# Attention's masked scores times v: two 64-column products side by side become one 128-column product

## The chip, the cores and the metric

The kernel runs on one core of one Trainium2 chip. The metric is the device time of one execution in microseconds (us). The kernel before took 642.28, 639.79 and 642.13 us in three runs, median 642.13; one more execution, taken by the hardware profiler, took 640.24 us and is the one the rows below come from. Engines are named as the profile names them: PE is TensorE's matmuls, PEld its weight loads, DVE VectorE, ACT ScalarE, POOL GpSimd, SP the engine that issues most DMAs.

## What is computed

Batch 4, 8 heads, 768 positions, head dimension 64. Attention goes in blocks with a decay of its own per head, and its output feeds a low-rank mixer with a two-layer perceptron:

```python
for b in range(nb):
    qb, kb, vb = (q[:, :, sl], k[:, :, sl], v[:, :, sl])
    intra = np.einsum('bhic,bhjc->bhij', qb, kb) * Dmask[None]
    intra = np.einsum('bhij,bhjd->bhid', intra, vb)
    inter = np.einsum('bhid,bhde->bhie', qb * lam_pow[None], kv_state)
    out[:, :, sl] = intra + inter
    kv_state = lam_block * kv_state + np.einsum('bhsd,bhse->bhde', kb_dec, vb)
...
h = xt @ U @ V
u = x + h.transpose(0, 2, 1)
ch = np.maximum(u @ w_ch1, 0.0) @ w_ch2
return (u + ch).astype(np.float32)
```

All of it is float32. The line that matters here is the second one of the loop: the masked scores times v.

## The kernel before

**Stages.** Attention takes blocks of 128 positions instead of the reference's 64 (same result, other grouping): 4 batches x 6 blocks = 24 steps, numbered s, with c = s % 6 the place in the batch. It lasts for about the first 118 us of the span. Then come the first layer of the perceptron and its second layer, long rows of matmuls with 128 columns of weights and 512 moving columns. Some of the mixer's work (mix, turn) and the preparation of the first weights are woven into the steps of attention.

**Order.** The order of the work in attention is written out by hand: a list of pieces for each step, run one after the other under a manual schedule. TensorE does its instructions in that order. A step, as TensorE sees it from step 7 on: the second half of earlier mixer work, the transposes of the next block's q and k (L416), intra (L514), state (L486), inter (L525), some mixer work (L618), the next step's scores (L463). Up to step 6 state comes ahead of intra. The last block of a batch (c = 5) has no state, the first (c = 0) no inter.

**The pieces around the change.**
- scores, L463: for each of 8 heads a product with 128 columns of weights and 128 moving columns over 64 rows; the two heads of a pair (x) lie in the two row halves of the array. The result goes to two banks of the matmul memory.
- masked, L472: VectorE multiplies the scores by the decay mask, one instruction for each x, into the tile sm: partitions are the positions j that are summed over, columns the 128 positions i of the block.
- intra, L514: masked scores times v, into the tile px. The weights are columns of sm, the moving operand is v of the head, 64 columns wide. The sum goes over 128 rows. The 128 positions i are taken in two halves, t = 0 and 1, each its own product with 64 columns of weights and its own 64 partitions of px: 2 x 4 x 2 = 16 products in a step.
- state, L486: keys times v for the running state, 8 products with 64 columns of weights over 128 rows.
- inter, L525: scaled queries times the state, added to px: 16 products of 64 rows by 64 columns, in quarters of the array.
- L531: ScalarE copies px out when inter is done.

The profile gives the part of the array that a matmul uses as rows*columns: 128*64 for L514 and L486, 64*64 for L525, 64*128 for L463 and L416, 128*128 for the perceptron.

A float32 product leaves two weight loads and two matmuls in the trace. So L514's 16 products in 24 steps are the 768 loads and 768 matmuls of its rows; transposes and the matmuls of type fp32r leave one of each.

Of the kernel before, what the change touches and what calls it, by code (L numbers as in the profile page):

```python
# [18 lines left out]
def kernel(  # L19
# [28 lines left out]
    nc = tc.nc  # L48

    B, H, S, D = q.shape  # L50
    HP = H // 2
# [258 lines left out]
    def two_banks(name, tag):  # L310
        return psf.tile([P, 2, N], FP32, tag=tag, name=name)
# [83 lines left out]
    half = [slice(0, D), slice(D, P)]  # L395
# [110 lines left out]
    def intra(s):  # L506

        st[s]["px"] = both = two_banks("px", "px")
        px = both[:, :, 0 : HP * D].rearrange("p x (a e) -> p x a e", a=HP)
        sm, vr, alone = st[s]["sm"], raw[s, "v"], s % NT == 0  # L510
        for x in range(2):
            for a in range(HP):
                for t in range(2):
                    nc.tensor.matmul(  # L514
                        out=px[half[t], x, a, :], lhsT=sm[:, x, a, half[t]],
                        rhs=vr[:, 2 * a + x, :], start=(a == 0), stop=(alone and a == HP - 1),
                    )

    def inter(s):

# [214 lines left out]
    def load_next(name, engine=nc.sync):  # L735
# [4 lines left out]
    run = {  # L740
        "prep": prep, "fade": fade, "scores": scores, "masked": masked, "inter": inter,
        "intra": intra, "state": state,
        "low": low, "low_rows": low_rows, "next_of_low": next_of_low, "mix": mix, "turn": turn,
        "mixed": mixed, "store": store, "next_v": next_v, "split": lambda s: splits.pop(s)(),
# [727 lines left out]
```

## Time and profile before

| what | value |
|---|---|
| median of three runs | 642.13 us |
| the profiled execution | 640.24 us |
| its span, first to last instruction | 638.5 us |
| TensorE matmuls busy, whole span | 628.4 us, 5197 records |
| weight loads busy, whole span | 529.0 us, 5197 records |
| VectorE, ScalarE, GpSimd busy | 463.0, 334.3, 147.0 us |
| granted TensorE clock | 1.0 |
| L514: matmul record, median | 222 ns |
| L514: idle time of PE just before it | 1.8 us in all |

The span is what the records cover; the execution's own time is 1.74 us longer. Busy time of matmuls is the union of their records, which overlap: a record of 222 ns does not mean that the next one starts 222 ns later. The start of one record to the start of the next of its kind says how fast they go.

### The profile page before, as it was taken

How to read it: one execution, taken by the hardware profiler on the slowest of the kernel's cores; microseconds unless marked ns; L12 is line 12 of the kernel's file. 1: busy time of each engine (PE TensorE's matmuls, PEld its weight loads, DVE VectorE, ACT ScalarE, POOL GpSimd, SP SyncE). 2: the span in 40 equal slices, each digit the busy share in tenths (PEclk: the TensorE clock that was granted, in tenths of full speed). 3: DMA queues.
4: the chain of work that ended last, by engine and by line, in shares of the span. 5: the costliest groups of instructions: out<-in, count | busy, mean ns of one | idle time of the engine just before them, and what ended most of it. 6: DMA issues, size and time to landing. Idle time of an engine off the chain costs nothing.

```text
span 638.5 us, 13622 instructions
## 1 busy us (share of the span) xinstructions
PE 628.4 (98%) x5197; PEld 529.0 (83%) x5197; DVE 463.0 (73%) x740; ACT 334.3 (52%) x615; POOL 147.0 (23%) x125
## 2 busy tenths in 40 slices
PE   8899999999999999999999999999999999999997
PEld 7888989888888888888888878888888888888886
DVE  6756778757888788797888799685674755855844
ACT  4675767445777777778777654232322322323220
POOL 4475959100000000000566500030110300300300
PEclk9999999999999999999999999999999999999999
DMA  9979996347798888855776696362363363532521
GB/s 230 244 186 269 233 248 163 135 175 268 260 354 281 280 306 290 292 195 190 250 232 229 227 332 216 112 225 95 113 216 99 127 203 93 190 131 99 182 83 66
DMA packets 141955, 129.61 MB, mean 203 GB/s; under 512 B 82562, under 2 KB 99970, under 8 KB 141890
## 3 DMA queue, kind: packets, MB, share of 16 engines
q1 hardware_dynamic: 116768, 122.32, 59.4%
q10 hardware_dynamic: 25122, 6.42, 4.5%
q8 instruction: 41, 0.67, 0.4%
q14 instruction: 24, 0.20, 0.1%
HBM read 79.04 MB, written 49.28 MB: 201 GB/s over the span
## 4 chain that ended last, share of the span: by engine, by line
PE 95%; ACT 2%; issue 1%; DMA 1%; DVE 1%; DVEq 0%; ACTq 0%
PE pz L958 24%; PE pz L1314 14%; PE pz L1312 14%; PE pd L1316 13%; PE z L958 4%; PE px L514 4%; PE pss L463 4%; PE p L958 3%; PE pz L889 2%; PE d L958 2%; PE px L525 2%; PE pqk L416 2%; PE c L958 2%; PE pkv L486 1%; PE pd L900 1%
## 5 line engine op out<-in xcount | busy, mean ns | idle before, releaser
L1296 ACT ACTIVATE m<-rm 128x512 fp32r<-128x512 f32 x96 | 60.6, 631 | 174.6 <-PE pd L1316 136.6
L1297 DVE SCALAR_TENSOR_TENSOR m<-rm,m 128x512 fp32r<-128x512 f32 x96 | 71.6, 747 | 82.1 <-ACT m L1296 82.1
L958 PE MATMUL pz<-u_hl,w 128*128 128x512 f32 x448 | 110.3, 389 | 0.0
L1312 PE MATMUL pz<-w_hl,m 128*128 128x512 f32 x264 | 102.7, 389 | 0.0
L1314 PE MATMUL pz<-w_hl,m 128*128 128x512 f32 x264 | 102.7, 389 | 0.0
L1316 PE MATMUL pd<-w_d,m 128*128 128x512 f32 (+1 forms) x267 | 101.4, 387 | 0.0
L958 PEld LDWEIGHTS pz<-u_hl,w 128*128 128x128 f32 x448 | 84.1, 188 | 17.4
L285 POOL TENSOR_TENSOR w<-w 128x512 fp32r<-128x512 f32 x29 | 40.5, 1415 | 211.4 <-DVE w L279 197.1
L1298 DVE SCALAR_TENSOR_TENSOR m<-m 128x512 fp32r<-128x512 f32 x96 | 74.9, 780 | 3.1
L1344 POOL TENSOR_TENSOR o<-o,u 128x512 f32<-128x512 f32 x20 | 29.8, 1519 | 199.1 <-DVE o L1340 199.1
L958 PE MATMUL pz<-u_d,w 128*128 128x512 f32 x224 | 59.9, 389 | 0.0
L1316 PEld LDWEIGHTS pd<-w_d,m 128*128 128x128 f32 x267 | 49.9, 188 | 10.3
L1312 PEld LDWEIGHTS pz<-w_hl,m 128*128 128x128 f32 x264 | 49.6, 188 | 10.3
L1314 PEld LDWEIGHTS pz<-w_hl,m 128*128 128x128 f32 x264 | 49.6, 188 | 10.2
L958 PEld LDWEIGHTS pz<-u_d,w 128*128 128x128 f32 x224 | 42.0, 188 | 8.8
L1312 PE MATMUL pz<-w,m 128*128 128x512 f32 x120 | 46.7, 389 | 0.0
L1316 PE MATMUL pd<-w,m 128*128 128x512 f32 x120 | 46.7, 389 | 0.0
L1314 PE MATMUL pz<-w,m 128*128 128x512 f32 x120 | 46.7, 389 | 0.0
L965 ACT ACTIVATE pz<-pz 128x512 f32<-128x512 f32 x56 | 32.5, 581 | 26.4 <-PE pz L958 26.4
L472 DVE TENSOR_TENSOR sm<-pss,mask 128x512 f32<-128x512 f32 x48 | 30.9, 686 | 19.8 <-PE pss L463 19.8
L969 ACT ACTIVATE r<-pz 128x512 f32<-128x512 f32 x56 | 33.2, 595 | 12.0 <-PE pz L958 11.4
L196 DVE SCALAR_TENSOR_TENSOR sc<-words,sc 128x512 uint32<-128x512 uint32 (+2 forms) x34 | 23.8, 700 | 17.6 <-ACT sc L178 17.6
(140 smaller groups left out, 1119.5 us busy)
## 6 DMA issues: line engine op xcount, KB each, us to landing
r_d<-r SPq DMA_DIRECT2D x96, 256.0 KB, 2.9
rm<-r_d SPq DMA_DIRECT2D x96, 256.0 KB, 2.6
words<-in_moe_w_ch_dram SPq DMA_DIRECT2D x30, 512.0 KB, 5.1
wf<-forms_d SPq DMA_DIRECT2D x56, 128.0 KB, 2.9
u_d<-x_nat SPq DMA_DIRECT2D x24, 256.0 KB, 4.2
u<-u_d SPq DMA_DIRECT2D x24, 256.0 KB, 4.5
qraw<-in_q_dram SPq DMA_DIRECT2D x23, 256.0 KB, 4.6
out_dram<-o SPq DMA_DIRECT2D x23, 256.0 KB, 2.0
```

The costliest lines, as they stand in the source:

```text
L285: engine.tensor_tensor(out=st["third"], in0=st["low"].bitcast(FP32), in1=st["hi"].bitcast(FP32), op=ALU.subtract,)
L472: nc.vector.tensor_tensor(out=sm[:, x], in0=pss[:, x], in1=mask[:, x], op=ALU.mult)
L958: nc.tensor.matmul(out=out, lhsT=weights, rhs=moving, start=start and i == 0, stop=i == len(pieces) - 1, skip_group_check=not start,)
L965: nc.scalar.mul(acc, acc, 1.0 + E)
L969: nc.scalar.mul(r, acc, 4096.0)
L1296: nc.scalar.activation(out=m[:, 0], in_=r, func=AF.Relu, scale=NEAR)
L1297: nc.vector.scalar_tensor_tensor(m[:, 1], r, 0.0, hi, ALU.max, ALU.subtract)
L1298: nc.vector.scalar_tensor_tensor(m[:, 2], hi, E, low, ALU.mult, ALU.subtract)
L1312: nc.tensor.matmul(out=pz, lhsT=m[:, 0, cols], rhs=hi, start=first, stop=False)
L1314: nc.tensor.matmul(out=pz, lhsT=m[:, 1, cols], rhs=low, start=False, stop=end)
L1316: nc.tensor.matmul(out=pd[:, part], lhsT=m[:, 2, cols], rhs=third[:, part], start=first, stop=end, skip_group_check=part.stop != C,)
L1344: nc.gpsimd.tensor_tensor(out=o, in0=o, in1=u, op=ALU.add)
```

## The change

The loop over the two halves t goes. Each product takes all 128 columns of sm for its head as weights and writes all 128 partitions of px. The moving operand, the order over x and a and the start and stop marks stay. A step has 8 products where it had 16; each uses the whole array (128*128) where each used one column half (128*64).

```diff
         for x in range(2):
             for a in range(HP):
-                for t in range(2):
-                    nc.tensor.matmul(
-                        out=px[half[t], x, a, :], lhsT=sm[:, x, a, half[t]],
-                        rhs=vr[:, 2 * a + x, :], start=(a == 0), stop=(alone and a == HP - 1),
-                    )
+                nc.tensor.matmul(
+                    out=px[:, x, a, :], lhsT=sm[:, x, a, :],
+                    rhs=vr[:, 2 * a + x, :], start=(a == 0), stop=(alone and a == HP - 1),
+                )
```

Nothing else of the kernel is changed; in the changed kernel the line of the product is L513, and later lines count one less.

## The prediction

> **What bounds the kernel now.** I read first how busy TensorE is by stage, then the chain of waits in the stage that holds the change, then that stage's weight loads and matmuls in order of time, and last the loads' durations by line. The first view gives busy time and records of each engine in four stretches (the third lies inside the second):
>
> ```profile
> core 0: us, PE busy (x) PEld busy (x) DVE busy (x) ACT busy (x) POOL busy (x), PEclk, DMA share, GB/s
> 0.00:118.00 118.00, 111.98 (x2873) 102.38 (x2877) 83.19 (x160) 73.17 (x168) 76.72 (x76) 1.00 0.88 215
> 118.00:372.00 254.00, 254.00 (x1174) 209.70 (x1167) 204.30 (x337) 184.70 (x322) 40.53 (x29) 1.00 0.75 256
> 220.00:310.00 90.00, 90.00 (x399) 74.53 (x398) 77.06 (x122) 69.67 (x118) 2.72 (x2) 1.00 0.76 257
> ```
>
> Attention is the first 118 us. TensorE is idle there for 118.00 - 111.98 = 6.0 us, and for nothing in the 254 us behind it. So whatever attention ends later moves the end of the kernel by as much; only those 6.0 us can swallow a delay. The chain of waits of this stretch, by line, says whose work it is:
>
> ```profile
> by line: PE px L514 19.7%; PE pss L463 19.5%; PE px L525 10.9%; PE pqk L416 9.3%; PE pkv L486 7.1%; PE pm L618 5.2%; DMA qraw<-in_q_dram 4.6%; issue 4.1%; PE pm L675 3.1%; PE pp L541 2.6%; PE idle L401 2.4%; PE pz L889 1.9%; ACT vp L772 1.6
> ```
>
> The line that is changed, L514, is on it with 19.7% of 118 us = 23 us, 0.97 us in each of 24 steps. What sets its pace shows in the order of time, weight loads (PEld) first, then matmuls (PE); each row is a run of like records with its start, its length and its count:
>
> ```profile
> 37.33 0.97 PEld L463 LDWEIGHTS pss<-qt,kt 64*128 64x128 f32 x16 [0.28 <-ACT kt L422]
> ...
> 44.07 1.01 PEld L514 LDWEIGHTS px<-vraw,sm 128*64 128x64 f32 x32
> 44.99 0.55 PEld L486 LDWEIGHTS pkv<-vraw,ks 128*64 128x64 f32 x16
> 45.62 0.56 PEld L525 LDWEIGHTS px<-kv,qs 64*64 64x64 f32 x32
> ```
>
> ```profile
> 35.57 0.69 PE L486 MATMUL pkv<-vraw,ks 128*64 128x64 f32 x16
> ...
> 37.33 1.16 PE L463 MATMUL pss<-qt,kt 64*128 64x128 f32 x16
> ...
> 41.93 1.05 PE L463 MATMUL pss<-qt,kt 64*128 64x128 f32 x16
> ...
> 45.05 0.64 PE L486 MATMUL pkv<-vraw,ks 128*64 128x64 f32 x16
> 45.62 0.69 PE L525 MATMUL px<-kv,qs 64*64 64x64 f32 x32
> ```
>
> L514's 16 float32 products of a step leave 32 loads and 32 matmuls, two records for each product. Products t=0 and t=1 use the two column halves of the array, and single records show the two 7 ns apart: they run side by side. 32 loads are 16 pairs; a load lasts 138 ns, so the pairs follow each other every (1010 - 138) / 15 = 58 ns. L525 puts four at once into quarters and keeps the same rhythm: (560 - 135) / 7, less the 20 ns over which four start, is 58 ns. So neither the number of records nor that of loads sets the 58 ns, and halving the number of products alone wins nothing. L463, with 128 weight columns in each of two row halves, goes at (970 - 188) / 7 = 112 ns.
>
> The loads' durations by line (minimum, median, maximum in ns):
>
> ```profile
> L541 PEld LDWEIGHTS pp<-x_nat,u_w x192: 106/110/110, 33.0 to 118.9; 128*32 128x32 f32 x192
> L525 PEld LDWEIGHTS px<-kv,qs x640: 129/135/135, 14.0 to 114.9; 64*64 64x64 f32 x160
> L514 PEld LDWEIGHTS px<-vraw,sm x768: 132/138/138, 9.1 to 114.3; 128*64 128x64 f32 x192
> L463 PEld LDWEIGHTS pss<-qt,kt x384: 182/188/330, 6.0 to 112.1; 64*128 64x128 f32 x192
> ```
>
> 32, 64 and 128 columns take 110, 138 and 188 ns: 0.78 to 0.88 ns for each further column, and the rows hardly count (L525 and L514). Where a group begins afresh, single records show the second load of a half 28, 55 and 109 ns behind the first for 32, 64 and 128 columns. So the weight path is held some 0.85 ns per column, 109 ns for 128; separate halves or quarters load at the same time.
>
> **The change, part by part.** (1) A product now has 128 columns of weights on the whole array, and 8 are left of 16: 16 records of each kind where 32 stood. They no longer pair up, so the row of 16 slots stays 16 slots long. A slot now holds a load of 128 columns against matmul work that took 58 ns. Its cost is not in this trace: no float32 load of 128 columns is followed by a matmul of only 64 moving columns on the full array. The low end is 58 ns (the load wholly hidden, L514's own rhythm), the high end 188 ns (the load's whole record, nothing hidden). I take L463's 112 ns: same type and columns, half the rows, which do not count in the durations; and 109 ns is the hold seen by itself. Of a step's 16 slots 15 are intervals: 15 x (112 - 58) = 0.81 us.
>
> A rule of the Trainium skill would make it worse. TensorE: Matmul & The Clock Gate, Part 3, The mechanism, lists as seen in traces that a weight load overlaps a matmul in flight only when it goes to another row group; on the whole array there is no other. By it a slot would be a load behind a matmul. This trace contradicts it: between 220 and 310 us every load and matmul takes the whole array, and loads are in flight for 74.53 of 90.00 us while matmuls are busy for all 90.00. With the overlap the sum stands as above; without it, it is the third rival's.
>
> (2) Changing the array's division costs time. From L486's first matmul at 45.05 to L525's at 45.62 are 0.57 us, where 8 pairs at 58 ns need 0.47: 0.09 us (0.094 by single records) lost in going over. The first interval of the new group is longer too: L486 lasts 0.69 us entered from another division and 0.64 entered from L514, 0.05 more; L463, with 128 columns, 1.16 against 1.05, 0.11 more. L514 and L486 shared one division (128*64) and now do not. In the 20 steps that have both, whichever comes first, that is one more crossing: 0.09 + 0.05 = 0.14 us, x 20 = 2.8 us. In every step the group of L514 begins with a load of 128 columns: 0.11 for 0.05, 0.06 us.
>
> (3) Nothing else moves: the DMAs, the semaphores waited for, VectorE's L472 and ScalarE's L531 stay in order. Behind L514 on TensorE stand L486 or L525, then the rest of the step, so all of it starts later. The second half of L514 waits for the second half of the masked scores; it comes later now, so that wait can only shrink. These engines have room: 83.19, 73.17 and 76.72 us busy of 118.
>
> Sum: 24 x (0.81 + 0.06) + 2.8 = 23.7 us.
>
> (4) What is given back. Part of the 6.0 us goes: two waits for q's loads early on, whose landing times don't follow TensorE, and the waits that the profile gives to nobody, 3.8 us of "issue" ahead of L514, L416, L525, L463 and L486. These may shrink because a quarter fewer records per microsecond are issued there. The first two are:
>
> ```profile
> 11.82 0.35 PEld L416 LDWEIGHTS pqk<-ident,qraw 64*128 64x128 f32 x8 [0.63 <-PE pss L463]
> ...
> 16.12 0.35 PEld L416 LDWEIGHTS pqk<-ident,qraw 64*128 64x128 f32 x8 [0.48 <-PE pss L463]
> ```
>
> I take back both, 1.1 us, and a quarter of the issue waits, 1.0. The ends are 0 and 6.0. That leaves 23.7 - 2.1 = +21.6 us. The profiled execution took 640.24 us (span 638.5); 640.24 + 21.6 = 661.8. The median of the three runs shown is 642.13, 1.9 above it, with one run below it; I put half of that on top: **662.7 us**.
>
> **The rivals.** First, the load is hidden or quicker than I say (no measurable change). For it: L416 loads 128 columns in 139 ns and its pairs go every 62 ns. Against: those are transposes, and L463, ordinary float32 like L514, takes 188 and 112. With 58 to 62 ns a slot the slots cost up to 24 x 15 x 4 ns = 1.4 us, the crossings 2.8 to 4.2, given back 2.1: about 643.
>
> Second, faster: the pace is set by issuing, so many ns for each record, and half the records of this line take half its time. It decides if a record costs 29 ns by itself (58 ns for two). It would save 24 x 15 x 29 ns = 10.4 us, less 2.8 for the crossings: about 632. Against it: L525's four records fit into the same 58 ns, 14.5 each.
>
> Third, loads do not overlap matmuls on the whole array: 112 + 58 = 170 ns a slot, 24 x 15 x 112 ns = 40.3 us, plus 4.2 for crossings, less 2.1: about 683. Against it is the stretch from 220 to 310 us.
>
> Fourth, transfers bound the stage (DMA share 0.88 over it), and all 6.0 us of idle time swallow delay: 640.24 + 23.7 - 6.0 = 658. Against: TensorE's own lines make up most of the chain, DMA qraw 4.6%.
>
> **How the numbers follow.** Forecast 0.83, first rival 0.06, second 0.03, third 0.04, fourth 0.04. The forecast's own spread: 109 to 119 ns a slot (the hold alone; 112 and the 7 ns by which two halves start apart, should a full load pay them one after the other) gives -1.1 to +2.5 us, what is given back -4 to +2, and the run taken for the sum +-1. So 655 to 669 us, which holds the fourth rival and leaves out the others. A difference under 0.5%, 3.2 us, can't be told from no change here: faster 0.03 (the second), same 0.05 and slower 0.92 (the first splits, nearly all of it same).
>
> **What would show it.** Right: L514's loads last 188 ns and start 112 ns apart, x16 a step; its group takes 1.8 us and not 0.93; where L486 follows it, L486 takes 0.69 us and starts 0.15 behind the last matmul; attention ends 21 to 24 us later and nothing after it changes. Wrong: loads of 138 ns or slots near 58 or 62 (first), near 29 (second), near 170 (third); or the group at 1.8 us but attention less than 18 us longer, with TensorE's idle time gone (fourth).

## The result and the profile after

The changed kernel took 656.83 us (median of four runs, 656.34 to 661.08), the kernel before in the same comparison 641.05 (639.79 to 642.28): 15.8 us more, a ratio of 1.0275 with a 95% interval of 1.0246 to 1.0304. The profiled executions stand at 640.24 and 656.34 us, 16.1 apart.

Busy time by stage, with attention now some 134 us long (columns as before):

```profile
core 0: us, PE busy (x) PEld busy (x) DVE busy (x) ACT busy (x) POOL busy (x), PEclk, DMA share, GB/s
0.00:135.00 135.00, 132.70 (x2525) 123.59 (x2529) 84.08 (x163) 74.30 (x169) 75.46 (x76) 1.00 0.78 190
135.00:388.00 253.00, 253.00 (x1142) 208.75 (x1131) 203.47 (x334) 183.85 (x320) 40.47 (x29) 1.00 0.74 255
```

All of the loss is in attention: the first matmul of the perceptron starts 16.0 us later by its single record (131.12 for 115.09), and from there to the end of the span both kernels take 523.4 us. Within attention the idle time fell from 6.0 us to 2.3. The chain of waits of the first 118 us, by line:

```profile
by line: PE px L513 34.5%; PE pss L463 20.8%; PE pqk L416 9.9%; PE px L524 9.0%; PE pkv L486 8.3%; PE pm L617 4.5%; PE pp L540 3.7%; DMA kraw<-in_k_dram 3.1%; PE pm L674 2.9%; PE px L486 1.0%; issue 0.9%; ACTq L817 0.4%; ACTq L337 0.4%
```

The changed line (L513 now) has gone from 19.7% to 34.5%, "issue" from 4.1% to 0.9%, and DMA qraw (4.6%) is gone. One step in order of time, weight loads and then matmuls, and the durations of the changed line:

```profile
48.10 1.86 PEld L513 LDWEIGHTS px<-vraw,sm 128*128 128x128 f32 x16
50.03 0.55 PEld L486 LDWEIGHTS pkv<-vraw,ks 128*64 128x64 f32 x16
```

```profile
48.10 2.00 PE L513 MATMUL px<-vraw,sm 128*128 128x64 f32 x16
50.03 0.69 PE L486 MATMUL pkv<-vraw,ks 128*64 128x64 f32 x16
...
53.41 0.44 PE L513 MATMUL px<-vraw,sm 128*128 128x64 f32 x2
```

```profile
L513 PEld LDWEIGHTS px<-vraw,sm x384: 186/192/193, 9.3 to 130.2; 128*128 128x128 f32 x192
```

There are 16 loads where 32 stood, each 192 ns long, one every (1860 - 192) / 15 = 111 ns. L486 behind them is entered from another division of the array and takes 0.69 us where it took 0.64. The step from L513 to L513 is 53.41 - 48.10 = 5.31 us; before, L514 to L514 was 48.38 - 44.07 = 4.31.

### The profile page after: what moved, and what is told of

Same layout as the page of the kernel before. It is cut to its first block, busy times and chain, and to the rows that moved or that the text cites. A ratio compares the mean times of both kernels' runs of the same rounds, so it can differ in the third digit from the quotient of the medians.

```text
span 654.5 us, 12848 instructions
## 1 busy us (share of the span) xinstructions
PE 648.2 (99%) x4813; PEld 549.4 (84%) x4813; DVE 463.2 (71%) x740; ACT 334.6 (51%) x615; POOL 145.7 (22%) x125
## 4 chain that ended last, share of the span: by engine, by line
PE 97%; DVE 1%; DMA 1%; issue 1%; ACT 0%; ACTq 0%; DVEq 0%
PE pz L957 23%; PE pz L1311 13%; PE pz L1313 13%; PE pd L1315 13%; PE px L513 7%; PE pss L463 4%; PE z L957 4%; PE p L957 3%; PE pz L888 2%; PE d L957 2%; PE px L524 2%; PE pqk L416 2%; PE pkv L486 2%; PE c L957 2%; PE pd L899 1%; PE pm L617 1%
## 5 line engine op out<-in xcount | busy, mean ns | idle before, releaser
L513 PE MATMUL px<-vraw,sm 128*128 128x64 f32 x384 | 47.8, 278 | 1.0 <-issue 0.7
L513 PEld LDWEIGHTS px<-vraw,sm 128*128 128x128 f32 x384 | 44.7, 192 | 2.8 <-issue 1.6
```

Of the source, the lines that this page charges most:

```text
L513: nc.tensor.matmul(out=px[:, x, a, :], lhsT=sm[:, x, a, :], rhs=vr[:, 2 * a + x, :], start=(a == 0), stop=(alone and a == HP - 1),)
```

## The experiments

A kernel below ran once, and its trace is of that run, unless a ratio is given with its time. The kernel before took 639.15 to 641.31 us beside them.

**What sets the slot: the load or the matmul.** Two kernels change only how many columns of v are streamed through the same 128-column weights. The first streams v twice, the second copy into an unread half of the bank:

```diff
+        px2 = both.rearrange("p x (two a e) -> p x two a e", two=2, a=HP)
-                    out=px[:, x, a, :], lhsT=sm[:, x, a, :],
-                    rhs=vr[:, 2 * a + x, :], start=(a == 0), stop=(alone and a == HP - 1),
+                    out=px2[:, x, :, a, :], lhsT=sm[:, x, a, :],
+                    rhs=vr[:, 2 * a + x, :].unsqueeze(1).broadcast_to([P, 2, D]),
+                    start=(a == 0), stop=(alone and a == HP - 1),
```

> The changed kernel with the moving operand doubled: v's 64 columns are streamed twice, the second copy into a half of the bank that nobody reads. Loads are as before. Theory (the load of 128 columns sets the slot, the matmul hides behind it): slots stay at 112 ns, L513's group at 1.72 us, time within 2 us of the changed kernel, about 657. Rival (the matmul on the whole array sets the slot): slots of some 220 ns, 24 x 15 x 108 ns = 39 us more, about 696. Second rival (load and matmul in series, 112 = 54 + 58): slots of some 165 ns, about 676.

The second streams 32 columns in 20 steps:

```diff
-        px = both[:, :, 0 : HP * D].rearrange("p x (a e) -> p x a e", a=HP)
+        at = 0 if s % NT == 0 else HP * D
+        px = both[:, :, at : at + HP * D].rearrange("p x (a e) -> p x a e", a=HP)
+        n = D if alone else D // 2
-                    out=px[:, x, a, :], lhsT=sm[:, x, a, :],
-                    rhs=vr[:, 2 * a + x, :], start=(a == 0), stop=(alone and a == HP - 1),
+                    out=px[:, x, a, 0:n], lhsT=sm[:, x, a, :],
+                    rhs=vr[:, 2 * a + x, 0:n], start=(a == 0), stop=(a == HP - 1),
...
-                        rhs=kv[s][half[x], a, :], start=False, stop=(a == HP - 1),
+                        rhs=kv[s][half[x], a, :], start=(a == 0), stop=(a == HP - 1),
```

> The changed kernel with 32 of v's 64 columns streamed in the 20 steps that have inter; the products go to the unread half of the bank, so masked scores times v is left out of the output in these steps. Theory (load sets the slot): 112 ns, group 1.72 us, about 657. Rival (matmul sets it): 56 to 60 ns, 20 x 15 x 54 ns = 16 us less, about 641. In series: about 85 ns, about 649.

Measured: 658.37 and 659.76 us. A step's weight loads in order of time, of the first kernel (128 columns streamed):

```profile
54.66 1.86 PEld L513 LDWEIGHTS px<-vraw,sm 128*128 128x128 f32 x16
```

and of the second (32 columns):

```profile
51.96 1.86 PEld L515 LDWEIGHTS px<-vraw,sm 128*128 128x128 f32 x16
```

The 16 loads take 1.86 us in both, as with 64 columns. A stream of 32, 64 or 128 columns costs the same: it lies wholly under the load, and the load sets the slot. Both rivals, that of a slow matmul and that of load and matmul in series, fall.

The microseconds over 657 have other sources. With 128 columns the first interval of each group is 213 ns by its single records where the changed kernel has 160, about 1 us in 20 steps. The second kernel lost 3.9 us ahead of the fifth step's scores, in steps such as this:

```profile
9.72 3.49 PEld L515 LDWEIGHTS px<-vraw,sm 128*128 128x128 f32 x16
```

Its loads are 213 ns apart there and 112 from 17.8 us on. The first clock record of its trace, full clock, stands at 17.69 us, that of the changed kernel's at 8.57. From the scores of the fifth step to the perceptron it takes 105.2 us, the changed kernel 105.6. In the traces of this document the first record of the full clock stands between 8.0 and 17.9 us, so single times can differ by some 4 us for this alone.

**Whether the load goes by its columns.** The changed kernel with 96 of the 128 weight columns in the same 20 steps, products to the unread half as above:

```diff
+        n = P if alone else 96
-                    out=px[:, x, a, :], lhsT=sm[:, x, a, :],
+                    out=px[0:n, x, a, :], lhsT=sm[:, x, a, 0:n],
```

> The changed kernel with 96 of the 128 weight columns loaded in the 20 steps that have inter; the products go to the unread half of the bank, so masked scores times v is left out of the output there. Theory (a load holds the weight path 0.85 ns for each column): slots of 82 to 85 ns, 20 x 15 x 28 ns = 8.4 us less than the changed kernel, about 648. Rival (the hold goes by the part of the array, 128 wide): 112 ns, about 657.

Measured: 649.18 us. The weight loads in order of time, and the duration of the line's loads (the maximum is of a step with 128):

```profile
51.55 1.43 PEld L515 LDWEIGHTS px<-vraw,sm 128*96 128x96 f32 x16
```

```profile
L515 PEld LDWEIGHTS px<-vraw,sm x384: 159/165/338, 10.2 to 123.2; 128*96 128x96 f32 x160, 128*128 128x128 f32 x32
```

That is (1430 - 165) / 15 = 84 ns a slot. 64, 96 and 128 columns go at 58, 85 and 112 ns by single records: some 0.85 ns for each further column, as the prediction had it. The Trainium skill, TensorE: Matmul & The Clock Gate, LDWEIGHTS, says columns / 1.2 in ns whatever the rows; by it 64, 96 and 128 columns are estimated at 53, 80 and 107 ns, and the slots measured here are 5 ns longer at each of the three.

**What set the pace before.** The kernel before with 32 columns of v streamed (edit as for full_moving_32, on the two-half loop), and with v streamed twice (as for full_moving_128):

> The kernel before (two column halves) with 32 of v's 64 columns streamed in the 20 steps that have inter; masked scores times v is left out of the output there. It asks what sets the 58 ns of the kernel before. Theory: a load of 64 columns holds its half for 55 ns, so pairs stay at 55 to 58 ns and the time at 641. Rival (streaming 64 columns sets it): pairs at some 30 ns, 20 x 15 x 28 ns = 8 us less, about 633.

> The kernel before (two column halves) with v's 64 columns streamed twice. Theory: load and stream are equally long before (55 ns held, 64 columns streamed), so doubling the stream makes pairs 109 to 112 ns as L541's with 128 moving columns are, 24 x 15 x 52 ns = 19 us more, less 5 to 7 of TensorE's idle time in attention: about 654. Rival (only the load matters, a stream of any length hides): pairs at 58 ns, about 641.

Measured: 650.16 and 654.38 us. Weight loads of a step, first with 32 columns streamed, then with 128:

```profile
53.34 1.02 PEld L516 LDWEIGHTS px<-vraw,sm 128*64 128x64 f32 x32
```

```profile
53.68 1.73 PEld L514 LDWEIGHTS px<-vraw,sm 128*64 128x64 f32 x32
```

With half the stream the pairs stay at 58 ns, (1020 - 138) / 15 = 59 by the row: the loads alone suffice for the pace of before. With twice the stream they go at 109 ns by single records, so the stream of before by itself is estimated at half of that, 55 ns. Before, load and stream were thus about equally long and hid each other, in both halves at once. The change doubled the load of a product and left its stream, and the load then sets the pace.

The first of the two kernels was expected at 641 and took 650, not by its slots but by two long waits and a lower clock behind each of them (last section). Matmuls in order of time:

```profile
24.30 0.22 PE L416 MATMUL pqk<-ident,kraw 64*128 64x64 f32 x1
28.11 0.41 PE L416 MATMUL pqk<-ident,kraw 64*128 64x64 f32 x7 [3.59 <-issue]
28.44 1.12 PE L486 MATMUL pkv<-vraw,ks 128*64 128x64 f32 x16
29.35 1.87 PE L516 MATMUL px<-vraw,sm 128*64 128x32 f32 x32
```

TensorE stands still for 3.59 us, and the profile names nothing that it waited for, in the middle of a row of like transposes. The kernel before waits at the very same place, and at others:

```profile
20.38 0.49 PE L463 MATMUL pss<-qt,kt 64*128 64x128 f32 x4 [0.48 <-issue]
...
25.59 0.40 PE L416 MATMUL pqk<-ident,kraw 64*128 64x64 f32 x7 [0.62 <-issue]
...
64.37 0.74 PE L514 MATMUL px<-vraw,sm 128*64 128x64 f32 x18 [0.78 <-issue]
```

Counted in TensorE's records (loads and matmuls together), such waits of the kernel before fall behind records 688, 939, 1445, 2708, 2962, 3972 and 4226, in steps of 251 to 254 and about their multiples. The semaphore instructions in TensorE's stream make up the difference: counted with them, the waits stand before instructions 705, 961, 1473, 2753, 3009, 4033 and 4289, all whole multiples of 256 apart, on one grid. The expectations below name 4664 in place of 1445; that was my mistake. 4664 is off this grid (438 behind 4226), at the border of L514 and L486, where a semaphore instruction of TensorE lasts until ScalarE's copy of k is done. The list of DMA queues of the kernel before in the first 118 us (packets, MB, share) has one queue, q8, that carries instructions at this rate:

```profile
q8 instruction: 23, 0.38, 1.2%
```

These are 23 packets of 16 KB, one for every 256 instructions of TensorE. The single packets in the trace show that the waits are for them: in each of the seven, TensorE went on 1.3 to 1.5 us after a packet of q8 had landed. The packets took 0.9 to 1.1 us; what differs is their start. It lies 2.2 to 3.3 us behind the crossing into the block before at the seven, and 0.2 to 2.2 us at the other 15 crossings up to 118 us. So the waits are for blocks of instructions. From start to start of TensorE's records they hold 4.3 us; only 2.7 of that counts as idle time of the matmuls, since a matmul's record, over 200 ns long, covers the beginning of each wait.

The Trainium skill, Runtime: NRT & Kernel Launch, Instruction fetch mechanics, gives blocks of 16 KiB or 256 instructions, and calls the crossing mostly hidden. The size agrees. Hidden it was at 15 of these 22 crossings; the other seven cost 0.4 to 1.0 us each, and single ones of halves_moving_32 3.8 and 2.6.

The changed kernel has no wait at such a place, and neither has the last one, halves_moving_128, which has all 5197 records of before at a slower pace. It is not the smaller number of records that took the waits away. A block lasts 5.6 us or more in the changed kernel, where the undisturbed ones of the kernel before last 4.3 to 5.4 within attention; its packets start at most 2.2 us behind the crossing and land 3.1 us or more ahead of need.

**Pace or transfers.** Where TensorE is slower, the transfers are spread too. To part the two, the kernel before got fewer transfers at its old pace:

```diff
         if waiting[name]:
-            load(name, waiting[name].pop(0), engine)
+            s = waiting[name].pop(0)
+            if name == "v" and s > 2:
+                raw[s, "v"] = kept_v[s % 3]
+                return
+            load(name, s, engine)
+            if name == "v":
+                kept_v.append(raw[s, "v"])
```

> The kernel before, v loaded for the first three steps only and these three tiles used again in all later ones: 5.5 MB and about a quarter of attention's transfer time less, no instruction of TensorE changed; the output is that of other v. It asks why TensorE's waits without a releaser went when it became slower. Theory (blocks of instructions come late because the transfer engines are full): the waits at records 688, 939, 2708, 2962, 3972, 4226, 4664 shrink from 4.5 us together to under 1.5, time 635 to 638. Rival (only the pace of the records counts, a block takes its time whatever else moves): same waits at the same records, 640 to 642.

Measured: 638.29 us, ratio 0.9963 (0.9942 to 0.9985) to the kernel before, which took 639.99 in that comparison. Of the seven waits on the grid five are gone; left are 0.48 us behind record 1445 and 0.38 behind 4227, 0.9 in place of 4.3. The wait behind 4664, which is not one of them, stays with 0.47, and a new one of 0.57 off the grid, for a transfer of the mixer's (vp), stands behind 3274. The transfer share of the first 118 us is 0.70, where it was 0.88, and the packets of instructions start 1.6 us behind the crossing in the median, where it was 2.0. The theory held on the whole; the time is 0.3 us above what was expected, and 1.7 of the 3.4 us of waits show in it.

Then slower kernels got more transfers, first all of v a second time (a tile nobody reads, loaded by ScalarE's queue; in the changed kernel, in halves_moving_128 and in the kernel before):

```diff
         raw[s, name] = t
+        if name == "v":
+            again = raw_pool.tile([P, H, D], FP32, tag="again", bufs=1, name="again")
+            nc.scalar.dma_start(
+                out=again, in_=source[b, :, c * P : (c + 1) * P, :].rearrange("h p d -> p h d")
+            )
```

> The changed kernel with every tile of v loaded a second time into a tile nobody reads: 6.3 MB more, transfer share in attention from 0.78 to about 0.95. It asks whether TensorE's waits for instructions are gone because its records come slower or because the transfers have more room. Theory (full transfer engines make blocks of instructions late): waits without a releaser come back at records some 256 apart, 2 to 6 us together, 659 to 663. Rival (only the pace of the records): none come back, 656 to 658; waits for q, k and v may come.

> The kernel with two column halves and v's columns streamed twice (all records of the kernel before, at a slower pace), with every tile of v loaded a second time into a tile nobody reads. Theory (full transfer engines): waits come back at the records of the kernel before (688, 939, 2708, 2962, 3972, 4226, 4664), 2 to 6 us together, 656 to 661. Rival (pace alone): none, 654 to 656.

> The kernel before with every tile of v loaded a second time into a tile nobody reads. Theory (full transfer engines): waits at more of the boundaries 256 records apart and longer ones, 6 to 15 us together where the kernel before has 4, time 643 to 655. Rival (pace alone): the waits of the kernel before, 640 to 643.

Measured: 667.39, 664.78 and 657.37 us. These answer little: the chain of the first 118 us of before_more_v reads

```profile
by line: DMA again<-in_v_dram 41.6%; PE pss L468 6.0%; PE px L519 4.3%; DMA words<-in_moe_w_ch_dram 4.2%; DMA u_d<-x_nat 4.0%; issue 4.0%; PE pp L546 3.9%; DMA qraw<-in_q_dram 3.4%; PE pm L623 3.3%; PE pkv L491 3.2%; PE pqk L421 3.0%; PE px
```

ScalarE waited in its queue for the added tile, so TensorE waited for data through ScalarE, and in none of the three does a wait over 0.3 us stand on the grid. With half of it, and two tiles in turn, the share in the first 134 us is 0.88, that of the kernel before in its 118:

```diff
+            again = raw_pool.tile([P, H // 2, D], FP32, tag="again", bufs=2, name="again")
+            engine.dma_start(
+                out=again,
+                in_=source[b, 0 : H // 2, c * P : (c + 1) * P, :].rearrange("h p d -> p h d"),
+            )
```

> As halves_128_more_v, but only half of each tile of v is loaded a second time, into two tiles in turn: 3.1 MB more, so that the transfer share of attention is about that of the kernel before (0.88) at a slower pace of TensorE's records, all 5197 of them. Theory (full transfer engines alone make blocks of instructions late): waits without a releaser at records 688, 939, 2708, 2962, 3972, 4226 or 4664, 2 to 4 us together. Rival (the pace decides at this share): none at these records, time 654 to 657.

> The changed kernel with half of each tile of v loaded a second time, into two tiles in turn: transfer share of attention about 0.88, as in the kernel before. Theory (full transfer engines alone): waits without a releaser at records some 256 apart, 2 to 4 us together, 659 to 661. Rival (the pace decides at this share): none, 656 to 659.

Measured: 658.53 and 661.33 us. In the first there is no wait behind the seven records, and one of 0.5 us on the grid, behind 1190; the rest of the added time is mostly waits for data, for q and through ScalarE, that follow the added load. The second has its own count of records and no wait at the crossings. Its 661.33 is no sign of the theory: 4.1 of the 5.0 us over the changed kernel's profiled execution lie ahead of the fifth step's scores, and its first record of the full clock stands at 17.89 us.

The changed kernel shows the same without any added load. Over the first 118 us its transfer share is 0.87; the 0.78 of its 135 us comes from the last 17, at 0.17:

```profile
0.00:118.00 118.00, 115.76 (x2216) 108.27 (x2216) 71.95 (x142) 66.86 (x154) 68.89 (x71) 1.00 0.87 209
```

So at the same share a slower pace leaves 0 to 0.5 us where the faster left 4.3 (and 7.6 in halves_moving_32); at the same pace, a smaller share leaves 0.9. Each of these is one execution. Both count: the pace sets when a block is needed, and a late start of its packet decides whether it is there. Why a packet starts late is not shown.

**The same change on another line.** The kernel before with inter (L525) on 128 columns, intra as it was:

```diff
-                for t in range(2):
-                    nc.tensor.matmul(
-                        out=px[half[t], x, a, :], lhsT=st[s]["qs"][half[x], a, half[t]],
-                        rhs=kv[s][half[x], a, :], start=False, stop=(a == HP - 1),
-                    )
+                nc.tensor.matmul(
+                    out=px[:, x, a, :], lhsT=st[s]["qs"][half[x], a, :],
+                    rhs=kv[s][half[x], a, :], start=False, stop=(a == HP - 1),
+                )
```

> The kernel before with the same change made to inter (L525) and not to intra: 8 products with 128 weight columns over 64 rows in place of 16 quarters, 32 records a step fewer on loads and matmuls each as 16 and 16. Theory: two row halves at 112 ns for 8 slots where four quarters took 58, +0.43 us a step, the crossing into L463 or L618 falls away, -0.20 us, so +4.6 us over 20 steps; the waits for instructions shrink by 2 to 4: 641 to 644, no clear difference. Rival (the larger tile is as quick): 632 to 636. Rival (crossings cost nothing, waits stay): 649 to 650.

Measured: 641.71 us, ratio 1.003 (1.0019 to 1.0041). Matmuls in order of time:

```profile
45.53 1.11 PE L524 MATMUL px<-kv,qs 64*128 64x64 f32 x16
46.47 1.11 PE L463 MATMUL pss<-qt,kt 64*128 64x128 f32 x16
...
50.05 1.11 PE L524 MATMUL px<-kv,qs 64*128 64x64 f32 x16
```

The group takes 1.11 us where L525 took 0.69, and L463 follows in the same division with no crossing. A step is 50.05 - 45.53 = 4.52 us, 0.21 more than 4.31; the forecast by the same prices was +0.43 - 0.20 = +0.23. Over 20 steps that is 4.2 us; the whole kernel lost 1.7 by the medians, the rest came back, and no wait on the grid of blocks is left in its trace. Its ten runs lie within 1.2 us; 19 runs of the kernel before in that comparison lie within 6.8 (638.05 to 644.83).

No version tried beats the kernel before with the same output.

## Why the prediction was right, and where it was off

- **Halving the number of products wins nothing by itself: right.** The 16 slots of a step stayed 16.
- **A slot of 112 ns, set by the load of 128 columns: right.** 112 by single records; the stream under it can be 32 to 128 columns without a change, and 96 columns give 85. The third rival, by which loads and matmuls don't overlap on the whole array, had slots of 170 ns; it fell with the 112, and with full_moving_128, where twice the stream left them at 112.
- **The crossings: right in sum.** The last matmul of L513 starts 205 ns ahead of the next group, where 112 is the slot: 0.09 us. L486 entered anew takes 0.05 more. Entering L513 costs no more than entering L514 did (first intervals of 160 and 107 ns, 48 and 49 over the slot), where the sum had 0.06; but the sixteenth slot, up to the crossing, is 0.05 longer too, and the sum counted 15. The two cancel. By rows a step with all pieces costs 5.31 - 4.31 = 1.00 us more; the prediction had 0.81 + 0.06 + 0.14 = 1.01. That holds for the 14 steps with state behind intra; the six with state ahead of it cost 0.94, the four without state 0.83. Together that is 23.0 us where the sum had 23.7.
- **What is given back: the term that was mis-sized.** "I take back both, 1.1 us, and a quarter of the issue waits, 1.0." Attention lost 16.0 us of the 23.0: 7.0 came back where 2.1 were forecast. Set against each other group by group, the two traces show all of it. The two early waits for q went, 1.1 us; the rows shown for them name L463 as the releaser, the waits of the matmuls (us in total, times, longest) name q's loads:

```profile
PE pqk L416 <- DMA qraw<-in_q_dram: 0.8, 2, 0.5
```

  The steps with the seven waits for blocks of instructions got back 4.5 us, the one with the wait ahead of L486 behind record 4664 0.5. The remaining 0.9 are short waits of L514 for the second half of the masked scores, some 0.1 each, and one for ScalarE's copy of k.
- **The bound of 6.0 us fell.** The prediction's "only those 6.0 us can swallow a delay" took idle time for waiting time. Idle time fell by 3.7 us and 7.0 came back, largely because part of each wait passes under the record of the matmul ahead of it.
- I read "issue" as something that shrinks with the number of records per microsecond, a quarter of it with a quarter fewer. Here it did not shrink in proportion: a block of instructions was either late or not, and at the slower pace none was. That the waits sit 250 records apart could have been read in the trace before.
- **The sign and the range.** Attention was to end 21 to 24 us later and ended 16.0 later, under the 18 that was named as a sign of the fourth rival. The 7.0 given back are more than the spread allowed for (2.1 and 4 more). The time, 656.83, lies in the range near its low end, by the range's width more than by the sum.
- **The fourth rival** had the idle time swallowing 6.0 us, 658: nearest in size, for another reason. It took the stage for bound by transfers; waits for data were the smaller part of what went, and 2.3 us of idle time stayed.
- Nothing behind attention changed, as forecast (523.4 us in both).

## What to carry to other kernels

Before two narrow products are merged into one wide one, see whether they already run side by side: the start of one record to the start of the next tells it, the count of records does not. Where few columns are streamed for each weight load, the load is the price, some 0.85 ns for each float32 column here. Two loads of 64 columns into separate halves of the array ran at the same time, 58 ns for the pair; one load of 128 columns took 112. Waits without a releaser that recur every 250 records or so are worth counting before a slowdown is priced: here a pace slower by 0.6 us or more a block removed nearly all of them. They are to be counted from start to start, since idle time leaves part of them out.

## What the runs showed that I had not expected

- Blocks of instructions come late in a dense stretch of small matmuls: 4.3 us in one execution of the kernel before, and single waits of 3.8 and 2.6 us from start to start in halves_moving_32.
- Such a wait can cost twice. Busy time and granted clock (the number ahead of the DMA share) of halves_moving_32 around its two long waits:

```profile
24.00:28.00 4.00, 0.52 (x13) 0.39 (x12) 1.87 (x4) 0.70 (x3) 0.00 (x0) 1.00 1.10 248
28.00:32.00 4.00, 3.89 (x87) 3.76 (x86) 0.42 (x1) 2.19 (x4) 2.73 (x3) 0.55 0.67 153
84.00:90.00 6.00, 3.99 (x102) 3.72 (x98) 4.04 (x7) 3.18 (x8) 4.75 (x4) 0.99 1.14 286
90.00:97.00 7.00, 6.64 (x109) 6.37 (x113) 3.29 (x5) 2.26 (x4) 3.22 (x3) 0.52 0.66 170
```

  The clock records of its trace have 0.5 for 6.83 us each, from 28.44 and from 89.88 us on. L516's pairs go at 107 ns there in place of 58 (its row at 29.35 lasts 1.87 us). If half of these 2 x 6.83 us is lost, an estimate, that is 6.8 us; with 7.6 us of waits in place of 4.3 it makes 10.1, and the span grew by 9.9. The Trainium skill, TensorE: Matmul & The Clock Gate, Part 1, has the clock halved after an idle window of about 3.4 us that runs free; a wait of 2.6 us was enough here.
- The kernel before spreads over 6.8 us from run to run, two kernels with fewer such waits over 1.5 (before_less_v) and 1.2 (before_inter_128). That the waits are the reason is not shown: the changed kernel, with none in its trace, spreads over 4.7 us, and the first record of the full clock, at 8.0 to 17.9 us in the traces, is another possible reason.
